# Reordering one step of a chunked recurrence: state products, block products, flags, scans and the decay of the state

## The chip, the cores and the metric

The kernel runs on one core of a Trainium2 chip. The metric is device time in microseconds of one execution. TensorE (PE, with its weight loads PEld), VectorE (DVE), ScalarE (ACT), GpSimd (POOL) and SyncE (SP, which issues nearly all DMAs) each work through their own list of instructions in order and wait for each other through semaphores.

## What is computed

Two stages follow each other. The first is a recurrence over 768 time steps for 4 x 8 heads with a 40 x 40 state each:

```
y[t]  = r[t] @ state
Sa    = state @ a[t]
state = state * w[t]  -  outer(Sa, b[t])  +  outer(v[t], k[t])
```

The second is a mixture of four attention experts on the output of the first (per expert a causal softmax attention of width 64, the two best experts of each token mixed by a gate). The change touches the first stage alone.

## The kernel before

**Chunks and windows.** The recurrence is not run step by step. Time is cut into 24 chunks of 32 (`NC`), and four chunks share one window of decays (`NW` = 6 windows). Within a chunk everything is a matrix product: the state products, a triangular 32 x 32 inverse for each head and chunk (`TT`), and masked products of r, k and v. Between windows the state is rescaled by the decay of a window (`PC`).

**A step.** The main loop runs `n` = 0 to 24 and, in each, walks through the list `MAIN`. Each letter is a method of `chunk(c)`, and the number beside it says for which chunk, counted from n:

```
MAIN = [("g", 0), ("f", -1), ("t", -1), ("k", 1), ("u", 0), ("v", 1), ("y", -1), ("z", -1), ("s", 0), ("w", 0)]
```

- g (L295): state times `AB`, accumulated in PSUM `pg`; ACT evicts it to `GT` (L296).
- f (L310): scores of the chunk before, into `pf`; DVE masks them into `FX` in two halves (L313).
- t (L318): transposed state, evicted by ACT into `SD` (L319).
- k (L276): the next chunk's keys, transposed through `pk`, evicted by ACT into `LS` (L277).
- u (L301): U = inverse times `GT`, into `pu`; ACT evicts it, turned in sign, into `R` in two halves (L303).
- v (L291): V's product for the next chunk, which starts its accumulation in `pg`.
- y (L322, L324): output of the chunk before, 64 products; z (L326) scales it on DVE into `XT`, and every second chunk is stored by DMA (L330).
- s (L336): update of the state in PSUM `ps`; DVE adds the old state (`ST`, L340). In the last chunk of a window DVE then multiplies the sum by `PC` (L345).
- w (L306): U transposed into `pu`, evicted by ACT into `VR` (L307).

PE takes these in the order of the list, so a product whose operand is late holds everything behind it. The state of chunk n, `ST`, is needed by g of the next step. `V1`, `R`, `RX` and `RB` have one buffer each; the loads for the next use are issued right behind the last reader (`LOADS`).

**Side work.** While one window is being run, the next is prepared. After each letter of `MAIN` (its place is counted from 0) the loop runs jobs from a table, `SIDE` (`SIDE1` for the first such window). A key of the table is a step counted from the first step of the window *before* the one that is prepared, and slashes part the ten places. The two halves (0 and 1, sixteen heads each) of a window are prepared apart. The letters are methods of `prep`, `mm` and `invert`:

- w, l, e: loads of `EW`, `EK` (into `KB`) and `EA` (into `AB`) by DMA.
- f, g: two flags on ACT over the decays (L176), each with one activation.
- a, b: suffix scan of the decays on DVE (L179) and what follows from it (L181, L182); s: prefix scan on DVE (L184).
- K, H: the two halves of the scaling of `KB` on POOL (L192); X: scaling of `AB` on POOL (L188). The small letters k and x are the same on DVE.
- m0, m1: the block products (L206) through `pk`, then `GB` and `GK` on DVE (L208, L209) and a mask on POOL (L210).
- L, t, T: the triangular inverses of the 16 x 16 blocks on DVE (L219, 28 small pieces in L227 and L229, L231, L232).
- B, D: operands for two more rounds of products, on ACT (L238); P and Q: these rounds, 128 products each through `pk` (L245), followed by an eviction on ACT (L248) and an addition on DVE (L252).

Window W's P, Q and its addition must be over before u of its first chunk. `START` lists what is done for windows 0 ahead of the loop, `AHEAD` what is then done already for window 1. `items` reads such a line.

In what follows the four steps of a window are called **kind 0 to kind 3** (n modulo 4). In the kernel before, kind 0 holds m0, m1 and L; kind 1 most of t, B and T; kind 2 D and P, and of the window after it the flags and scans of half 0; kind 3 Q, and the scans, flags and scalings of half 1 and the scaling of half 0.

Of the kernel before, what the change touches and what calls it, by code (L numbers as in the profile page):

```python
# [21 lines left out]
NW, NC = 6, 24  # L22

SIDE = {
    -3: "/////////0w",
    -2: "//0f0g0a//0l1l/0b0s1w",
    -1: "0e1e0K0H0X//1f1g1a/1b//1s1K1H1X",
    0: "/////m0/m1//L/t6",
    1: "//t4/t4/t4/t6///t4/TB",
    2: "D/////P",  # L30
    3: "/////Q",
}
START = "x0 0w 0l 0e 1w 1l 1e x1 c0 0a 0b 0f 0g 0k 0s 0x 1a 1b 1f 1g m0 1k 1s 1x x2 m1 L B k0 t28 T D P Q"
AHEAD = "0w 0l 1l 0e 1e"

SIDE1 = {
    0: "//0f0g0a0b0K0H///0s0X1w////1f1g1a1b1K1H",
    1: "/1s1X////m0///m1/L",
    2: "t4/t4/t4/t4/t4/t4/t4//T/B",
    3: "D//P///Q",  # L40
}


# [37 lines left out]
def recurrence(tc, ctx, I, xT, FL, CM, early, tail=None):  # L81
# [80 lines left out]
    def prep(w, a):  # L162
# [26 lines left out]
        def kmul(e, k):  # L189
            for t in two:  # L190
                x = kb[0:104, :, :, t, 32 * k:32 * k + 32]
                e.tensor_tensor(x, x, sv[:, :, 1:33].rearrange("p (x t c) n -> p x t c n", t=2, c=4)[:, :, t], op=OP.mult)  # L192
        return dict(w=lambda: load(EW, "EW"), e=load_a, l=lambda: load(kb.rearrange("p x c t n -> p (x c t n)"), "EK"),
                    f=lambda: flag(0), g=lambda: flag(1), a=suf, b=per, s=pre, x=lambda: amul(V), X=lambda: amul(PL),
                    k=lambda: (kmul(V, 0), kmul(V, 1)), K=lambda: kmul(PL, 0), H=lambda: kmul(PL, 1))

    def mm(w, a):

# [80 lines left out]
    def chunk(c):  # L279
# [45 lines left out]
        def s_z():  # L325
            V.tensor_tensor(xt[:, :, 32 * (cw % 2):32 * (cw % 2) + 32], PF[0:104].rearrange("p (i n) -> p i n", n=32),  # L326
                            SC[w % 3].rearrange("p (i c) n -> p i c n", c=4)[:, :, cw, 0:32], op=OP.mult)
            if cw % 2:
                for r in two:
                    SY.dma_start(xT.rearrange("b (h e) t -> (b h) e t", e=40)[16 * r:16 * r + 16, :, 32 * c - 32:32 * c + 32].rearrange("h e t -> e h t"),  # L330
                                 xt[rows(r)])
        def s_s():
            if c == NC - 1:
                return
            for x, r in heads:
                T.matmul(PS[rows(r), x // 4, 80 * (x % 4):80 * (x % 4) + 80], ls[:, x, r], r2[:, :, x, r], start=True, stop=True)  # L336
            pv = PS[0:104, :, 0:320]
            o, i = (x.rearrange("p (b x) t d -> p b (x t d)", b=2) for x in (st1, st0))
            if c:
                V.tensor_tensor(o, i, pv, op=OP.add)  # L340
            else:
                V.tensor_copy(o, pv)
            if cw == 3:
                o = st1.rearrange("p x t d -> p (x t) d")
                V.tensor_tensor(o, o, PC[(w + 1) % 3][:, :, None].to_broadcast([104, 16, 40]), op=OP.mult)  # L345
# [507 lines left out]
```

## Time and profile before

| | us |
|---|---|
| median of 3 runs | 710.42 (707.84 to 717.12) |
| the profiled execution | 711.22 |
| its span, first to last instruction | 709.4 |
| PE busy | 553.9 (78%) |
| DVE busy | 473.5 (67%) |
| ACT busy | 336.3 (47%) |
| POOL busy | 252.7 (36%) |

The profiled execution took 711.22 us, 1.8 us more than its span. The recurrence fills the first 447 us of the span: the window's set-up up to about 62 us, steps 0 to 3 up to 147.5 us, four full windows of steps up to 403.5 us, and the last window. The second stage takes the remaining 262 us. Sums over the whole span therefore mix stages, and the stages are looked at one by one. PEclk is the clock that was granted to TensorE, as a share of full speed.

### The profile page before, as it was taken

To read this page: it belongs to the slowest core of one execution; us is meant where nothing else is said; L and a number is where in the kernel's file an instruction comes from. 1 tells how busy PE (TensorE), PEld (TensorE's weight loads), DVE (VectorE), ACT (ScalarE), POOL (GpSimd) and SP (SyncE) were. 2 spreads that over 40 slices of the span, in tenths; PEclk is the share of its full clock that TensorE was granted. 3 is DMA by queue.
4 is the path that set the end of the run, shared out by engine and by line. 5 is a ranking of instruction groups with operands and counts; after the bars stand their busy time and mean duration, and the time that the engine had idled before them with its cause. 6 is when DMAs were issued, how large, how long until landed. Compare 5 with 4: busy or idle time off the path is not lost.

```text
span 709.4 us, 26350 instructions
## 1 busy us (share of the span) xinstructions
PE 553.9 (78%) x11497; PEld 506.1 (71%) x11497; DVE 473.5 (67%) x974; ACT 336.3 (47%) x702; POOL 252.7 (36%) x233
## 2 busy tenths in 40 slices
PE   0336573888859787868889998699889988999996
PEld 0325473887859677868778887688779877888784
DVE  8871459448643945673483324599999899689793
ACT  3022413424522641353234345267577777777783
POOL 7500762521262047122610001135545345333640
PEclk9999688889988997998798999999999999999999
DMA  5203423413541462254221262431121212201101
GB/s 164 66 0 86 142 66 109 121 40 91 165 108 42 114 175 63 69 142 128 55 77 40 70 191 73 127 101 46 52 80 41 75 45 57 79 1 45 57 1 61
DMA packets 42268, 57.92 MB, mean 82 GB/s; under 512 B 19808, under 2 KB 33376, under 8 KB 40224
## 3 DMA queue, kind: packets, MB, share of 16 engines
q1 hardware_dynamic: 42000, 56.05, 28.3%
q8 instruction: 92, 1.51, 0.9%
q14 instruction: 32, 0.26, 0.1%
q10 hardware_dynamic: 144, 0.10, 0.1%
HBM read 41.98 MB, written 7.86 MB: 70 GB/s over the span
## 4 chain that ended last, share of the span: by engine, by line
PE 32%; DVE 13%; ACT 4%; issue 4%; DMA 2%; SPq 0%; DVEq 0%; ACTq 0%
PE pt L610 4%; PE ot L735 3%; PE sc L690 3%; PE pt L746 3%; PE pt L720 3%; PE pk L245 3%; DVE m L700 2%; PE pf L322 2%; PE pg L295 2%; PE pf L310 2%; DVE qs L619 2%; ACT P L701 2%; PE pf L324 1%; DVE pt L724 1%; PE ps L318 1%
## 5 line engine op out<-in xcount | busy, mean ns | idle before, releaser
L712 POOL TENSOR_TENSOR P<-P,m 128x128 f32<-128x128 f32 (+2 forms) x96 | 89.2, 950 | 115.7 <-DVE m L708 62.0
L192 POOL TENSOR_TENSOR KB<-KB,SUF 104x512 f32<-104x512 f32 x40 | 54.8, 1401 | 99.5 <-DMA KB<-in_EK 88.4
L307 ACT ACTIVATE VR<-pu 80x1024 f32<-80x1024 f32 x24 | 24.5, 1020 | 132.4 <-PE pu L306 132.4
L701 ACT ACTIVATE P<-sc,m 128x128 f32<-128x128 f32 (+2 forms) x96 | 60.8, 634 | 27.5 <-DVE m L700 17.1
L690 PE MATMUL sc<-ks,qs 128*128 128x384 f32 (+4 forms) x256 | 62.5, 347 | 4.8 <-ACT P L701 2.8
L735 PE MATMUL ot<-pt,vv 128*128 128x256 f32 (+1 forms) x384 | 60.3, 289 | 6.3 <-DVE ots L741 6.1
L188 POOL TENSOR_TENSOR AB<-AB,SC 40x1024 f32<-40x1024 f32 x20 | 44.7, 2233 | 51.0 <-DMA AB<-in_EA 41.8
L724 DVE TENSOR_TENSOR pt<-pt,pt 128x384 fp32r<-128x384 f32 (+1 forms) x96 | 58.9, 618 | 5.3 <-ACT pt L723 3.5
L700 DVE TENSOR_REDUCE m<-sc 128x1 f32<-128x128 f32 (+2 forms) x96 | 58.7, 615 | 0.5
L735 PEld LDWEIGHTS ot<-pt,vv 128*128 128x128 f32 x384 | 50.8, 189 | 10.4 <-DVE ots L741 9.1
L295 PE MATMUL pg<-ST,AB 104*64 104x40 f32 x736 | 29.9, 247 | 34.2 <-DVE ST L340 20.7
L723 ACT ACTIVATE pt<-pt 128x384 fp32r<-128x384 f32 (+1 forms) x96 | 52.0, 544 | 9.8 <-PE pt L720 8.3
L206 PE MATMUL pk<-KB,AB 104*64 104x64 f32 x768 | 30.9, 250 | 32.7 <-DMA AB<-in_EA 19.6
L313 DVE TENSOR_TENSOR FX<-pf,CM 64x512 f32<-64x512 f32 x48 | 32.9, 684 | 35.4 <-PE pf L310 34.9
L720 PE MATMUL pt<-CM,P 128*128 128x128 f32 x336 | 52.9, 275 | 3.8 <-DVE qs L619 2.6
L295 PEld LDWEIGHTS pg<-ST,AB 104*64 104x64 f32 x736 | 27.0, 155 | 37.6 <-DVE ST L340 23.1
L206 PEld LDWEIGHTS pk<-KB,AB 104*64 104x64 f32 x768 | 29.4, 164 | 33.5 <-issue 19.7
L322 PE MATMUL pf<-FX,LS 128*40 128x64 f32 x768 | 48.7, 225 | 1.7 <-issue 1.1
L324 PE MATMUL pf<-RX,SD 80*40 80x64 f32 x736 | 47.2, 222 | 3.1 <-issue 3.1
L690 PEld LDWEIGHTS sc<-ks,qs 128*128 128x128 f32 x256 | 40.3, 190 | 8.3 <-ACT P L701 7.6
L610 PE MATMUL pt<-xh,wq 128*128 128x384 f32 x192 | 42.3, 355 | 4.7 <-DVE qs L619 4.5
L322 PEld LDWEIGHTS pf<-FX,LS 128*40 128x40 f32 x768 | 41.0, 118 | 4.1 <-issue 2.4
(140 smaller groups left out, 1362.3 us busy)
## 6 DMA issues: line engine op xcount, KB each, us to landing
KB<-in_EK SPq DMA_DIRECT2D x24, 320.0 KB
AB<-in_EA SPq DMA_DIRECT2D x24, 320.0 KB
ks<-ks SPq DMA_DIRECT2D x32, 192.0 KB
V<-in_V SPq DMA_DIRECT2D x24, 160.0 KB
R<-in_VX SPq DMA_DIRECT2D x48, 80.0 KB
RX<-in_RX SPq DMA_DIRECT2D x48, 80.0 KB
RB<-in_RB SPq DMA_DIRECT2D x48, 80.0 KB
xT<-XT SPq DMA_DIRECT2D x24, 160.0 KB
```

The source lines that it names most:

```text
L192: e.tensor_tensor(x, x, sv[:, :, 1:33].rearrange("p (x t c) n -> p x t c n", t=2, c=4)[:, :, t], op=OP.mult)
L206: T.matmul(PK[rows(t, 64), x // 2, y:y + 64], ab[:, n], kb[0:104, 4 * a + x, c, t], start=True, stop=True)
L295: T.matmul(pg[rows(t, 64), x], ab[:, 4 * (2 * x + t) + cw], st0[:, x, t], start=False, stop=True, skip_group_check=True)
L322: T.matmul(pf[rows(r), x], ls[:, x, r], FX[:, :, x, r], start=True, stop=c == 0)
L610: T.matmul(p, w, x, start=(j == 0), stop=(j == len(prs) - 1))
L690: T.matmul(ps[:, c, 0:cw], QS[b][:, e, o], KS[b][:, e, z, k], start=(z == 0), stop=(z == 1 and not last), skip_group_check=True)
L700: V.tensor_reduce(m[:, 0, t:t + 1], ps[:, 0:ch, 0:cw], axis=AX.XY, op=OP.max, negate=True)
L701: later(DE, lambda: A.activation(pv, ps[:, 0:ch, 0:cw], AF.Exp, bias=m[:, 0, t:t + 1], accum_out=m[:, 1, t:t + 1]))
L712: PL.tensor_tensor(P[:, 0:n], P[:, 0:n], m[:, 3, t:t + 1].to_broadcast([128, n]), op=OP.mult)
L720: T.transpose(p[:, 128 * y:128 * y + 128], st["P"][t][:, 128 * c:128 * c + 128], ident)
L724: later(DL, lambda: V.tensor_tensor(l, p[:, 0:n], f32(h), op=OP.subtract))
L735: T.matmul(po[:, 128:256] if one else po, VV[b][:, k, e].rearrange("p a b -> p (a b)"), PT[:, 256 * k:256 * k + (128 if one else 256)], st ...
```

## The change

It does five things.

1. In `MAIN`, v moves from behind u to the end of the step.
2. The tables are rewritten: m0 stands behind u, and m1, P and Q stand behind v, at the end of a step; the flags f and g stand behind u (place 5, behind y; ACT's eviction of U is ahead of them); the four long scans of a window get four places in kinds 2, 3 and 0, and one of the scalings of `KB` moves from POOL to DVE (the new letter p); t is done in two pieces of 14.
3. `AHEAD` holds most of the preparation of window 1's half 0, and it stands in front of P and Q of window 0 and of the load of `V1` for chunk 1.
4. At the end of a window, the decay is applied to the old state (new method q, behind y) and to the new part in PSUM apart, and the two are then added.
5. The line numbers behind the insertion move: L336 becomes L342, L340 becomes L349, L345 becomes L333 (twice) and L347.

```diff
 SIDE = {
...
-    0: "/////m0/m1//L/t6",
-    1: "//t4/t4/t4/t6///t4/TB",
-    2: "D/////P",
-    3: "/////Q",
+    0: "1s1H1X////m0/1f1g////m1L",
+    1: "/t14////B///t14",
+    2: "/T////D////P",
+    3: "/////////Q",
...
-AHEAD = "0w 0l 1l 0e 1e"
+AHEAD = "0w 0l 1l 0e 1e 0a 0b 0f 0g 0s 0K 0H 0X 1w"
...
+        def gauge(o, x):
+            V.tensor_tensor(o, x, PC[(w + 1) % 3].rearrange("p (b i) -> p b i", b=2)[:, :, :, None].to_broadcast([104, 2, 8, 40]), op=OP.mult)
+        def s_q():
+            if cw == 3 and c < NC - 1:
+                o, i = (x.rearrange("p (b x) t d -> p b (x t) d", b=2) for x in (st1, st0))
+                gauge(o, i)
...
-            if c:
+            if cw == 3:
+                gauge(pv.rearrange("p b (i d) -> p b i d", d=40), pv.rearrange("p b (i d) -> p b i d", d=40))
+                V.tensor_tensor(o, o, pv, op=OP.add)
+            elif c:
                 V.tensor_tensor(o, i, pv, op=OP.add)
             else:
                 V.tensor_copy(o, pv)
-            if cw == 3:
-                o = st1.rearrange("p x t d -> p (x t) d")
-                V.tensor_tensor(o, o, PC[(w + 1) % 3][:, :, None].to_broadcast([104, 16, 40]), op=OP.mult)
...
-    MAIN = [("g", 0), ("f", -1), ("t", -1), ("k", 1), ("u", 0), ("v", 1), ("y", -1), ("z", -1), ("s", 0), ("w", 0)]
+    MAIN = [("g", 0), ("f", -1), ("t", -1), ("k", 1), ("u", 0), ("y", -1), ("z", -1), ("s", 0), ("w", 0), ("v", 1)]
...
     units[0]["v"]()
+    for f in items(1, AHEAD, None, None) + items(0, "PQ", inv, None):
+        f()
     load_c(1, 0)
-    for f in items(1, AHEAD, None, None):
-        f()
...
                 units[n + d][x]()
+                if x == "y":
+                    units[n]["q"]() if n < NC else None
```

What this does to the order on the engines is seen at three places. On PE, from a step of kind 2 in the steady windows, before (rows without y, which ends just ahead of the first of them in both kernels):

```order
366 L306 MATMUL pu<-CM,R_111 80x64 x16
367 L295 MATMUL pg<-ST_116,AB_98 64x40 x16
368 L310 MATMUL pf<-RB_113,VR_112 64x64 x16
369 L318 MATMUL ps<-CM,ST_117 80x104 x8
370 L276 MATMUL pk<-CM,KB_100 128x104 x8
371 L301 MATMUL pu<-GT_119,TT_106 32x40 x32
372 L291 MATMUL pg<-V_105,GK_103 32x40 x32
373 L245 MATMUL pk<-TT_107,BB_89 64x64 x58
```

and now, from the end of a step of kind 2 into the next step:

```order
404 L342 MATMUL ps<-R_111,LS_109 40x80 x16
405 L306 MATMUL pu<-CM,R_111 80x64 x16
406 L291 MATMUL pg<-V_105,GK_103 32x40 x32
407 L245 MATMUL pk<-TT_107,BB_89 64x64 x58
...
411 L295 MATMUL pg<-ST_117,AB_98 64x40 x16
412 L310 MATMUL pf<-RB_113,VR_112 64x64 x16
```

V's product (L291) and P (L245) stood between u (L301) and y; they now stand between s (L342) and the next g (L295). On ACT, a step of kind 2 before (JK is what the flags write, R the eviction of U):

```order
97 L319 ACTIVATE SD_118<-ps 80x640
98 L176 ACTIVATE JK_90,FL<-EW_82,CM 104x1024 x2
99 L277 ACTIVATE LS_108<-pk 128x640
100 L303 ACTIVATE R_111<-pu 32x640 x2
101 L248 ACTIVATE MT_86<-pk 128x512
102 L307 ACTIVATE VR_112<-pu 80x1024
```

and now:

```order
100 L319 ACTIVATE SD_118<-ps 80x640
101 L277 ACTIVATE LS_108<-pk 128x640
102 L303 ACTIVATE R_111<-pu 32x640 x2
103 L238 ACTIVATE DB_88<-DD_87,CM 128x32x16 x2
104 L176 ACTIVATE JK_90,FL<-EW_82,CM 104x1024
105 L307 ACTIVATE VR_112<-pu 80x1024
106 L248 ACTIVATE MT_86<-pk 128x512
```

The flags, which stood ahead of the evictions of the keys (LS) and of U (R), now stand behind both. On DVE, a step of kind 3 before:

```order
227 L313 TENSOR_TENSOR FX_115<-pf,CM 64x512 x2
228 L179 SCALAR_TENSOR_TENSOR SUF_84<-EW_82,D_81 104x1056
...
231 L252 TENSOR_TENSOR TT_107<-TT_107,pk 128x32x16
232 L184 SCALAR_TENSOR_TENSOR SC_96<-EW_82,D1P_85 104x1056
233 L326 TENSOR_TENSOR XT_120<-pf,SC_97 104x16x32
234 L340 TENSOR_TENSOR ST_116<-ST_117,ps 104x640
235 L345 TENSOR_TENSOR ST_116<-ST_116,PC_92 104x640
```

and now, up to the first DVE work of the next step:

```order
230 L313 TENSOR_TENSOR FX_115<-pf,CM 64x512 x2
231 L184 SCALAR_TENSOR_TENSOR SC_96<-EW_82,D1P_85 104x1056
232 L333 TENSOR_TENSOR ST_116<-ST_117,PC_92 104x640
233 L326 TENSOR_TENSOR XT_120<-pf,SC_97 104x16x32
234 L333 TENSOR_TENSOR ps<-ps,PC_92 104x2x320
235 L347 TENSOR_TENSOR ST_116<-ST_116,ps 104x640
236 L179 SCALAR_TENSOR_TENSOR SUF_84<-EW_82,D_81 104x1056
...
239 L192 TENSOR_TENSOR KB_100<-KB_100,SUF_84 104x16x32 x2
240 L252 TENSOR_TENSOR TT_107<-TT_107,pk 128x32x16
241 L184 SCALAR_TENSOR_TENSOR SC_96<-EW_82,D1P_85 104x1056
```

A scan (L179) and the addition to the inverse (L252) stood ahead of the new state; one scan (L184, of the other half) still does, the rest now follows it, and there is one DVE instruction more at the state (two in L333, one in L347, for two before) and two more for the scaling of `KB` (L192).

More of the change, by code (lines that the diff above doesn't have):

```diff
@@ L24 @@
 SIDE = {
-    -3: "/////////0w",
-    -2: "//0f0g0a//0l1l/0b0s1w",
-    -1: "0e1e0K0H0X//1f1g1a/1b//1s1K1H1X",
-    0: "/////m0/m1//L/t6",
-    1: "//t4/t4/t4/t6///t4/TB",
-    2: "D/////P",
-    3: "/////Q",
-}
-START = "x0 0w 0l 0e 1w 1l 1e x1 c0 0a 0b 0f 0g 0k 0s 0x 1a 1b 1f 1g m0 1k 1s 1x x2 m1 L B k0 t28 T D P Q"
-AHEAD = "0w 0l 1l 0e 1e"
+    -3: "0w/////0f",
+    -2: "///0l1l//0g////0a0b0K0H",
+    -1: "0e1e/0s0X1w///////1a1b1p",
+    0: "1s1H1X////m0/1f1g////m1L",
+    1: "/t14////B///t14",
+    2: "/T////D////P",
+    3: "/////////Q",
+}
+START = "x0 0w 0l 0e 1w 1l 1e x1 c0 0a 0b 0f 0g 0k 0s 0x 1a 1b 1f 1g m0 1k 1s 1x x2 m1 L B k0 t28 T D"
+AHEAD = "0w 0l 1l 0e 1e 0a 0b 0f 0g 0s 0K 0H 0X 1w"
 SIDE1 = {
[L37 to L40, printed above, removed]
+    0: "1a1b1K1H//1s1X//m0/1f1g",
+    1: "////m1/L/t4//t14",
+    2: "/t10T/////B///D",
+    3: "////P/////Q",
 }
@@ L194, in prep @@
                     f=lambda: flag(0), g=lambda: flag(1), a=suf, b=per, s=pre, x=lambda: amul(V), X=lambda: amul(PL),
-                    k=lambda: (kmul(V, 0), kmul(V, 1)), K=lambda: kmul(PL, 0), H=lambda: kmul(PL, 1))
+                    k=lambda: (kmul(V, 0), kmul(V, 1)), p=lambda: kmul(V, 0), K=lambda: kmul(PL, 0), H=lambda: kmul(PL, 1))
     def mm(w, a):
@@ L342, in s_s @@
                 V.tensor_copy(o, pv)
-            if cw == 3:
-                o = st1.rearrange("p x t d -> p (x t) d")
-                V.tensor_tensor(o, o, PC[(w + 1) % 3][:, :, None].to_broadcast([104, 16, 40]), op=OP.mult)
-        return dict(v=s_v, g=s_g, u=s_u, w=s_w, t=s_t, y=s_y, z=s_z, s=s_s, f=s_f)
+        return dict(v=s_v, g=s_g, u=s_u, w=s_w, t=s_t, y=s_y, z=s_z, s=s_s, f=s_f, q=s_q)
     jobs = {}
-    MAIN = [("g", 0), ("f", -1), ("t", -1), ("k", 1), ("u", 0), ("v", 1), ("y", -1), ("z", -1), ("s", 0), ("w", 0)]
+    MAIN = [("g", 0), ("f", -1), ("t", -1), ("k", 1), ("u", 0), ("y", -1), ("z", -1), ("s", 0), ("w", 0), ("v", 1)]
     def at(n, s, *fs):
```

## The prediction

> **What bounds the kernel now.** I cut the span at the starts of g in steps 0, 4, 8, 12, 16 and 20 and asked for each engine's busy time and the granted clock in each stretch. The columns are the length, then the busy time of PE, PEld, DVE, ACT and POOL with the number of instructions, the granted clock, the DMA share and GB/s.
>
> ```profile
> 62.00:147.50 85.50, 50.79 (x1513) 46.91 (x1498) 51.48 (x67) 28.38 (x43) 40.61 (x28) 0.82 0.39 112
> 147.50:212.60 65.10, 51.81 (x1666) 49.13 (x1666) 37.41 (x61) 25.01 (x37) 21.84 (x17) 0.90 0.39 104
> 212.60:277.30 64.70, 51.64 (x1664) 48.56 (x1664) 39.26 (x61) 24.90 (x37) 23.29 (x17) 0.92 0.39 105
> 277.30:343.50 66.20, 53.20 (x1666) 50.35 (x1666) 38.08 (x61) 24.92 (x37) 20.18 (x15) 0.89 0.39 103
> 343.50:403.50 60.00, 54.30 (x1664) 51.25 (x1664) 26.66 (x53) 20.89 (x29) 8.19 (x7) 0.87 0.21 56
> 403.50:447.50 44.00, 37.49 (x1280) 34.34 (x1280) 16.62 (x25) 19.14 (x27) 4.05 (x12) 1.00 0.40 114
> 447.50:709.40 261.90, 235.03 (x1617) 206.66 (x1617) 220.51 (x581) 181.95 (x477) 110.01 (x122) 0.99 0.21 59
> ```
>
> A window of four steps costs 60 to 66 us, with PE busy for 52 to 54 of them and nothing else above 40. So PE's list sets the pace, and it loses time in two ways: by waiting, and by the clock, which is 0.87 to 0.92 there and 1.00 in the last window. The 262 us behind 447.5 belong to the second stage, which the change leaves alone. Next the waits of PE (in sum, times, longest), in the four windows:
>
> ```profile
> PE pg L295 <- DVE ST L345: 13.5, 5, 4.3
> PE pk L245 <- ACT LS L277: 11.0, 6, 2.0
> PE pg L295 <- DVE ST L340: 11.0, 12, 2.0
> PE pk L245 <- issue: 6.8, 6, 2.9
> PE pf L324 <- issue: 3.1, 3, 1.5
> ```
>
> and in steps 0 to 3:
>
> ```profile
> PE pg L295 <- DVE ST L340: 8.6, 1, 8.6
> PE ps L336 <- ACT R L303: 8.0, 2, 7.2
> PE pu L301 <- ACT GT L296: 6.9, 1, 6.9
> PE pk L206 <- POOL AB L188: 3.5, 1, 3.5
> ```
>
> In the windows 24.5 us go to g waiting for the new state (13.5 + 11.0) and 11.0 us to P and Q waiting for the eviction LS, which stands behind two flags on ACT. "issue" is time for which the profile knows no releaser.
>
> The clock falls just behind such waits. Two waits from the order of time, and the stretches at half clock behind them:
>
> ```profile
> 263.47 1.28 PE L245 MATMUL pk<-MT,DB 64*64 64x64 f32 x26 [1.81 <-ACT LS L277]
> 277.33 1.70 PE L295 MATMUL pg<-ST,AB 104*64 104x40 f32 x32 [4.30 <-DVE ST L345]
> 264.00:267.40 3.40, 2.99 (x58) 2.80 (x55) 0.00 (x0) 0.62 (x1) 3.33 (x2) 0.50 0.67 177
> 277.70:284.50 6.80, 6.80 (x128) 6.43 (x127) 1.38 (x2) 1.84 (x3) 1.61 (x1) 0.50 0.10 27
> ```
>
> A wait of 1.81 us is followed by 3.4 us at half clock, one of 4.30 us by 6.8 us, in which PE is busy throughout. From the PEclk column, the time at half clock is 2 x (1 - clock) x length: 13.0 + 10.4 + 14.6 + 15.6 = 53.6 us in the four windows. In the two stretches PE is busy for 88 and 100% of it; with 80 to 90% everywhere, full clock would save 21 to 24 us, and I take 22. [...]
>
> **The price of a step on PE.** A step without side work, with nothing but the letters, in order of time:
>
> ```profile
> 413.66 1.13 PE L295 MATMUL pg<-ST,AB 104*64 104x40 f32 x32 [0.40 <-DVE ST L340]
> 414.62 1.13 PE L310 MATMUL pf<-RB,VR 80*64 80x64 f32 x32
> 415.68 0.91 PE L318 MATMUL ps<-CM,ST 104*80 104x104 f32 x8
> 416.43 0.88 PE L276 MATMUL pk<-CM,KB 104*128 104x104 f32 x8
> 417.23 0.77 PE L301 MATMUL pu<-GT,TT 32*32 32x40 f32 x63
> 417.83 0.79 PE L291 MATMUL pg<-V,GK 32*32 32x40 f32 x63
> 418.55 0.31 PE L322 MATMUL pf<-FX,LS 128*40 128x64 f32 x2
> 420.51 0.23 PE L336 MATMUL ps<-R,LS 128*40 128x80 f32 x1
> 421.90 0.65 PE L306 MATMUL pu<-CM,R 64*80 64x64 f32 x16
> 412.79 0.82 DVE L340 TENSOR_TENSOR ST<-ST,ps 104x640 f32<-104x640 f32 x1 [1.58 <-PE ps L336]
> 415.80 1.41 DVE L313 TENSOR_TENSOR FX<-pf,CM 64x512 f32<-64x512 f32 x2 [2.19 <-PE pf L310]
> ```
>
> From start to start: g 0.96, f 1.06, t 0.75, k 0.80, u 0.60, v 0.72, y 1.96, s 1.39, w 0.65, in sum 8.9 us, and 0.40 of wait for the state. Side work of a window:
>
> ```profile
> 155.69 2.09 PE L206 MATMUL pk<-KB,AB 104*64 104x64 f32 x64
> 182.71 3.91 PE L245 MATMUL pk<-TT,BB 64*64 64x64 f32 x128 [2.05 <-ACT LS L277]
> ```
>
> Less an overlap of 0.2 with what follows, m0 and m1 take 1.9 each; P takes 3.9 here; I take 4.2 for it and for Q, since other instances hold short pauses (6 of them in the list above). A window without any wait at full clock is 4 x 8.9 + 3.8 + 8.4 = **47.8 us**.
>
> **What the edits do, walked through one window.** Prices of the side work, by line (least, median and longest of one in ns, or busy us and mean ns of one):
>
> ```profile
> L345 DVE TENSOR_TENSOR ST<-ST,PC x5: 825/1629/2440, 145.8 to 402.7; 104x640 f32<-104x640 f32 x5
> L184 DVE TENSOR_TENSOR_SCAN SC<-EW,D1P x11: 2350/2358/3404, 14.6 to 337.4; 104x1056 f32<-104x1056 f32 x11
> L192 DVE TENSOR_TENSOR KB<-KB,SUF x8: 651/684/1748, 12.1 to 27.4; 104x512 f32<-104x512 f32 x8
> L219 DVE STREAM_TRANSPOSE MT<-GB 128x1024 f32<-128x1024 f32 x4 | 7.9, 1985 | 0.0
> L227 DVE TENSOR_TENSOR TP<-MT 128x112 f32<-128x112 f32 x12 | 3.3, 273 | 0.4
> L176 ACT ACTIVATE JK<-EW,CM 104x1024 bf16<-104x1024 f32 x22 | 25.2, 1145 | 12.8 <-DMA EW<-in_EW 12.4
> L188 POOL TENSOR_TENSOR AB<-AB,SC 40x1024 f32<-40x1024 f32 x13 | 29.5, 2272 | 31.3 <-DMA AB<-in_EA 28.1 <-PE ps L336 2.7
> ```
>
> *v behind w.* The state needs about 1.0 us behind s (0.82 of L340 and two hand-overs). w alone, 0.65, did not cover it; w and v, 1.37, do, and where P, Q or m1 follow, 2 to 4 us more. The 0.40 of a step without side work goes. Nothing is paid for v's new place: its `V1` load has a whole step either way, and its accumulation in `pg` starts behind GT's eviction.
>
> *Flags behind U's eviction, P and Q at the end.* LS and R no longer wait for two flags (L176, 1.15 us each, with a short read behind each some 2.6), and P and Q no longer stand between U and s. The 11.0 us go. The flags now precede VR on ACT, but w starts 4.0 us behind u's start (u, y and s), and R's two halves, each like a half of L313, end some 2.1 us behind it, which leaves room for one flag and most of the second.
>
> *Decay apart.* The product with the old state runs behind y, beside s. Behind s stand two instructions as before, now with PSUM operands: I take 0.82 each, the price of L340 (the bounds are 0.69, an eviction like half of L313, and the 2.44 of L345 at its longest). That is 1.7 us, and w, v and Q (5.6 us on PE) hide all of it; without that cover it would be the wait of 13.5 us again. A third instruction adds 0.8 us to DVE's list.
>
> *Walk, with 0 at g of kind 1.* An instruction of 512 columns on DVE (L208, L209, z) is taken as half of L313, 0.7, and T as one and a half of L219. L208, L209 and L219 behind m1 end at 3.5, FX at 4.9; y could start at 4.2, so PE **waits 0.8**. The first 14 pieces of t, half of 28 at up to 0.27, end at 8.8, z (0.7) at 9.5, the state at 10.3; s and w, v end at 9.7: **waits 0.7**. Kind 2 starts at 10.4; the second 14 hold DVE to 14.2, FX ends at 15.6, y could start at 14.6: **waits 1.1**. T (3.0) and z end at 19.4, the state at 20.2; P runs until 24.5. Kind 3: FX, the scan (2.4), the decayed old state, z and the two at the state end at 33.5; the next scan, its small followers and p at 38.5; Q at 37.5. Kind 0: the last scan ends at 42, FX at 43.5; m0 takes PE until 43.4: **waits 0.1**. `AB` of half 1 is ready on POOL at 46.5 (two of L188 behind the scan), m1 is due at 48. So: 47.8 + 2.7 = **50.5 us**. To this come the pauses without a releaser (6.8 + 3.1, with the small ones some 12 us in four windows): 3 us each (a little of which is in P's 4.2 already), **53.5**. The last of the four windows has no scans, and I take 51.
>
> *Clock.* Waits of 1.1 us and less: the last window has such ones, and ran at 1.00. I take full clock.
>
> [...]
>
> **The sum.** Four windows: 256.0 us before; 3 x 53.5 + 51 = 211.5 after: **-44.5**. Counter-check by what goes: 24.5 + 11.0 + 22 - 4 x 2.7 = 46.7.
>
> Steps 0 to 3: 85.5 us before. In the old order the loads of window 1 stand behind the load of `V1`, which waits for v; flags, scans and scalings follow late, and the four waits above, 27.0 us, are their price. Now these loads and half 0's work run beside P and Q of window 0. Walking on PE: 4 x 8.9 less what chunk 0 lacks (t, half of y, g: 4), 3.8, 8.4 and some 9 us of waits for half 1's scans and POOL's scalings in steps 0 and 1 give 53. DVE's 51.48, less half 0's scans (5.6) and plus 2.4, gives a floor of 48. PEclk 0.82 says that gaps there bring half clock, so I take 57.5: **-28** (bounds 0, since no load or scan comes later than before, and -37).
>
> Last window: 0.4 x 4: **-2**, rounded. In sum -74.5: 711.2 - 74.5 = 636.7. The median of the runs shown lies 0.8 below the profiled execution, which gives **636 us** (635.9).
>
> **Rivals.**
>
> 1. *DVE becomes the bound.* Its list grows from 39 to 41.7 us per window, and in kinds 3 and 0 it has no gap for 20 us. If scans and scalings are stretched by 1 us each beside POOL (9 instructions, 3.4 instead of 2.36 as in L184's longest), and every stretch lands on y, a window is 60 (the last 58), the start gives 20, and the sum is -18 - 20 - 2: about **670 us**. Against it: in kind 0 m0 covers 1.9 us. [...]
>
> 2. *The waits go, half clock stays.* If gaps of 1 us in succession are enough for it, the 22 us stay and the start gives 24: -22.5 - 24 - 2, **663 us**. Against it stands the last window at 1.00.
>
> 3. *Better still.* Pauses without a releaser shrink, since the products are spread more evenly, and the start reaches its floor: 3 x 51 + 49 and -37: **618 us**.
>
> 4. *Slower: half 1 comes late to m1.* m1, P and Q now stand ahead of g, in the list that carries the state. If POOL's scaling of half 1 (behind EK, EA, two scans, the decay) is later than 48 in the walk, PE stands, and everything with it; the slack is 1.5 us. The 74.5 us would be spent if each of five windows stood for 15 us beyond it. L188's row has 28.1 us of POOL waiting for EA's loads, which is 7 a window, but ahead of half 0's scaling, 12 us before m0. At 20 us per window: 636 + 100, **735 us**.
>
> 5. *Nothing happens.* P, Q, m0 and m1 remain in one list, and if a wait is only carried to the next letter, the time stays at **708**. Against it: every removed wait has work of another engine behind it in the walk.
>
> **Chances and range.** Forecast (625 to 652) 0.55; DVE-bound 0.15; half clock 0.10; better 0.13; nothing 0.04; slower 0.03. The range from 613 to 672 takes in the first four but their outer ends, and leaves out less than 2 in 10. About 2% (14 us) is what a measurement of this kernel can tell from no change: faster by more 0.93, within it 0.04, slower 0.03.
>
> **What would show it.** In the new profile: L245 with no wait for LS; L295's waits for the state near zero in kinds 0 and 3 and below 1 us in kinds 1 and 2; PEclk near 1.00 from step 4 on; windows of 51 to 56 us; step 4 starting at 115 to 125 us; the second stage again at 262. Wrong it would be if y (L322) waits for FX by more than 1.5 us a step, if m1 (L206) waits for `AB`, or if f waits for VR behind the flags.

## The result: 664.7 us, and what the profile after shows

| | before | after |
|---|---|---|
| median in the same comparison, us | 709.84 (707.84 to 717.12) | 664.74 (656.58 to 673.17) |
| ratio after / before, with its 95% interval | | 0.927 (0.914 to 0.940) |
| the profiled execution, us | 711.22 | 656.58 |

The ratio compares the faster executions of each kernel alone, which is why it is not the quotient of the two medians (0.936). By it the kernel is 7.3% faster. 636 us was predicted, with a range from 613 to 672. In a later comparison the changed kernel took 658.42 us (653.25 to 662.11), so a difference of some 6 us between numbers of two comparisons means nothing here.

First the same cut as before, at the starts of g in steps 4, 8, 12, 16 and 20 (columns as in the prediction: length, busy time of PE, PEld, DVE, ACT and POOL, granted clock, DMA share, GB/s). The first row holds steps 0 to 3, the last the second stage:

```profile
60.00:122.70 62.70, 52.42 (x1529) 49.27 (x1526) 41.96 (x64) 24.03 (x34) 28.93 (x20) 0.81 0.35 98
122.70:179.30 56.60, 50.55 (x1667) 47.55 (x1665) 41.15 (x65) 25.84 (x37) 19.96 (x15) 0.94 0.43 120
179.30:230.80 51.50, 47.40 (x1668) 44.66 (x1664) 35.81 (x61) 25.85 (x37) 16.83 (x13) 1.00 0.49 131
230.80:293.90 63.10, 51.78 (x1669) 48.70 (x1666) 41.28 (x65) 25.88 (x37) 19.47 (x14) 0.92 0.41 108
293.90:348.60 54.70, 49.10 (x1667) 46.21 (x1666) 34.13 (x60) 23.61 (x33) 10.10 (x8) 0.97 0.24 64
348.60:390.40 41.80, 36.89 (x1217) 33.87 (x1216) 16.16 (x24) 18.61 (x27) 3.45 (x4) 0.96 0.42 117
390.40:654.70 264.30, 237.73 (x1681) 208.49 (x1681) 221.07 (x584) 182.70 (x478) 110.67 (x131) 0.99 0.21 58
```

Step 4 starts at 122.7 instead of 147.5 us, a gain of 24.8. The four windows take 225.9 instead of 256.0 us, a gain of 30.1. The cut between the last window and the second stage does not fall on the same instruction in both kernels (1217 products ahead of it here, 1280 before), so these two are taken together: 306.1 instead of 305.9 us, no gain. In sum this is 54.7 us between the two profiled executions, and 74.5 were predicted. Of the 19.8 us that are missing, 14.4 lie in the four windows, where 44.5 were expected, 3.2 in steps 0 to 3, and 2.2 in what follows the windows. The median lies another 8 us above the profiled execution (664.74 against 656.58), and no profile shows where. The four windows are not alike: one took 51.5 us at full clock, another 63.1 at 0.92.

The waits of PE in these four windows (sum, times, longest):

```profile
PE pg L291 <- issue: 5.3, 3, 4.2
PE pk L276 <- DVE TT L252: 4.5, 2, 2.3
PE pf L322 <- DVE FX L313: 3.9, 7, 0.7
PE pu L306 <- issue: 3.2, 1, 3.2
PE pg L295 <- DVE ST L349: 2.9, 4, 0.8
PE pk L245 <- issue: 2.9, 3, 1.4
PE ps L342 <- issue: 1.9, 3, 0.9
PE pk L206 <- issue: 0.7, 1, 0.7
PE pu L301 <- issue: 0.7, 1, 0.7
PE pf L310 <- issue: 0.5, 1, 0.5
```

The waits that the change aimed at are gone. The 24.5 us of g for the state have become 2.9, once a window, and P and Q do not wait for LS at all (11.0 before). What is left is mostly "issue", 15.2 us in sum (5.3 + 3.2 + 2.9 + 1.9 + 0.7 + 0.7 + 0.5), and a wait that was not there before: k, 4.5 us, for the addition L252.

**What stands behind "issue".** The longest pause, with the instructions of PE around it in order of time, and the row of the load that SP had issued ahead of it:

```profile
262.62 1.42 SPq L170 DMA_DIRECT2D KB<-in_EK  x4
268.07 0.56 PE L291 MATMUL pg<-V,GK 32*32 32x40 f32 x39
272.87 0.43 PE L291 MATMUL pg<-V,GK 32*32 32x40 f32 x25 [4.24 <-issue]
```

and the stretch behind it, from the windows view (clock 0.50):

```profile
273.40:276.80 3.40, 3.40 (x69) 3.40 (x69) 0.00 (x0) 0.00 (x0) 2.29 (x3) 0.50 0.68 174
```

The pause falls in the middle of v, after 39 of its 64 products. All 64 have the same kinds of operands, and those of the other 25 were there: it is not data that PE lacks. Half clock begins right behind the pause. The page of the profile lists the DMA queues (packets, MB, share of 16 engines), and two of them carry instructions:

```profile
q8 instruction: 92, 1.51, 1.0%
q14 instruction: 32, 0.26, 0.1%
```

q8 is PE's: the same page counts 22,994 products and weight loads (11,497 each), which is 250 for each of its 92 packets. These packets are 16 KB each (1.51 MB in all), and in the trace's DMA records their starts in the recurrence lie about 4 us apart, 52 of them in the four windows. Here are the starts around the pause (us), from these records:

```
253.86  257.68  261.10  270.28  274.60  277.97
```

Between 261.10 and 270.28 none starts for 9.2 us, and in this time, at 262.62, SP issued the load of `EK` (four pieces of 320 KB). PE runs out of its list at 268.6 and goes on 2.6 us after the next packet started. The second longest pause, 3.2 us in w at 168.4, has the same picture: four pieces of `EA` issued from 161.34 on, and no instruction packet from 161.38 to 168.93.

That it is the list that runs out is seen from where the pauses stand. If PE's instructions are counted in the order of the trace (weight loads, products and the waits of its sequencer), all 13 pauses of the list above lie a multiple of 256 instructions apart, to within one. Each stands between two blocks of 16 KB (16,384 bytes, 64 for an instruction), whatever letter is being run, and PE goes on 2.2 to 2.9 us after the start of a packet. A packet starts when PE has begun the block before: 1.1 us later in the median of the four windows, but 5.2 and 4.4 us later at the two longest pauses. A block of side work is passed in 3.9 us (the 128 products of P with their weight loads), so even the usual 1.1 and 2.2 to 2.9 us leave little over. The 12 pauses that the kernel before has in its four windows stand between blocks as well.

**What stands behind k's wait.** SP's issues and DVE's rows from a step of kind 3 into the next, in order of time, and k at the end:

```profile
217.43 1.45 SPq L173 DMA_DIRECT2D AB<-in_EA  x4
220.02 2.36 DVE L184 TENSOR_TENSOR_SCAN SC<-EW,D1P 104x1056 f32<-104x1056 f32 x1
222.44 0.66 SPq L170 DMA_DIRECT2D EW<-in_EW  x2
230.30 2.36 DVE L179 TENSOR_TENSOR_SCAN SUF<-EW,D 104x1056 f32<-104x1056 f32 x1 [3.66 <-DMA EW<-in_EW]
233.02 3.10 DVE L192 TENSOR_TENSOR KB<-KB,SUF 104x512 f32<-104x512 f32 x2
236.04 0.67 DVE L252 TENSOR_TENSOR TT<-TT,pk 128x512 f32<-128x512 f32 x1
236.77 1.65 PE L276 MATMUL pk<-CM,KB 104*128 104x104 f32 x8 [2.32 <-DVE TT L252]
```

`EW` has one buffer, so SP issues the load of its half 1 when the scan 0s (L184) has read half 0, at 222.4. That is behind the four pieces of `EA`, and the scan 1a (L179) stands on DVE for 3.66 us until it has landed. The scaling p and then Q's addition L252 come late by as much, and k, whose PSUM buffer `pk` L252 reads, waits 2.32 us. In the four windows these waits of the scan are 11.5 us (three times), and two of them reach k; before there were none.

### The profile page after: what moved, and what is told of

It is laid out like the page before. It is cut to its first block, busy times and chain, and to the rows that moved or that the text cites. A ratio compares the mean times of both kernels' runs of the same rounds, so it can differ in the third digit from the quotient of the medians.

```text
span 654.7 us, 26365 instructions
## 1 busy us (share of the span) xinstructions
PE 544.8 (83%) x11497; PEld 496.8 (76%) x11497; DVE 480.6 (73%) x987; ACT 340.3 (52%) x702; POOL 241.2 (37%) x225
## 3 DMA queue, kind: packets, MB, share of 16 engines
q8 instruction: 92, 1.51, 1.0%
## 4 chain that ended last, share of the span: by engine, by line
PE 53%; DVE 26%; issue 8%; ACT 5%; DMA 4%; SPq 0%; DVEq 0%; ACTq 0%
PE pk L245 6%; PE ot L743 4%; PE pk L206 4%; PE pt L618 4%; PE pf L322 4%; PE pt L728 3%; PE sc L698 3%; PE pt L754 3%; PE ps L342 3%; PE pf L324 3%; PE pf L310 2%; DVE m L708 2%; PE pg L295 2%; DMA EW<-in_EW 2%; ACT P L709 2%
## 5 line engine op out<-in xcount | busy, mean ns | idle before, releaser
L192 POOL TENSOR_TENSOR KB<-KB,SUF 104x512 f32<-104x512 f32 x32 | 42.9, 1368 | 108.2 <-DVE SUF L179 83.3
L743 PEld LDWEIGHTS ot<-pt,vv 128*128 128x128 f32 x384 | 50.8, 189 | 11.1 <-DVE ots L749 9.2
L188 POOL TENSOR_TENSOR AB<-AB,SC 40x1024 f32<-40x1024 f32 x20 | 44.9, 2245 | 36.0 <-DVE SC L184 16.9
L731 ACT ACTIVATE pt<-pt 128x384 fp32r<-128x384 f32 (+1 forms) x96 | 52.0, 544 | 10.2 <-PE pt L728 8.8
L307 ACT ACTIVATE VR<-pu 80x1024 f32<-80x1024 f32 x24 | 24.5, 1021 | 42.6 <-PE pu L306 42.5
L296 ACT ACTIVATE GT<-pg 128x320 f32<-128x320 f32 x24 | 10.5, 437 | 63.0 <-PE pg L295 63.0
L728 PEld LDWEIGHTS pt<-CM,P 128*128 128x128 f32 x336 | 36.7, 141 | 7.5 <-issue 3.2
```

What stands on the lines that cost most here:

```text
L728: T.transpose(p[:, 128 * y:128 * y + 128], st["P"][t][:, 128 * c:128 * c + 128], ident)
L731: A.activation(h, p[:, 0:n], AF.Copy)
L743: T.matmul(po[:, 128:256] if one else po, VV[b][:, k, e].rearrange("p a b -> p (a b)"), PT[:, 256 * k:256 * k + (128 if one else 256)], st ...
```

## The experiments

The theory on which they were chosen: the sum of the prediction holds part by part, and what is missing comes from the bursts of loads. All times of the first four kernels are from one comparison, in which before took 712.47 us.

**Flags back in their places.**

```diff
-    -3: "0w/////0f",
-    -2: "///0l1l//0g////0a0b0K0H",
-    -1: "0e1e/0s0X1w///////1a1b1p",
-    0: "1s1H1X////m0/1f1g////m1L",
+    -3: "0w",
+    -2: "//0f0g/0l1l//////0a0b0K0H",
+    -1: "0e1e/0s0X1w/1f1g//////1a1b1p",
+    0: "1s1H1X////m0/////m1L",
```

> The changed kernel, with the flags of windows 2 to 5 put back to their old places in kinds 2 and 3, behind t and so ahead of the evictions of the keys (LS) and of U (R); all else as changed. My theory (each edit is worth the waits that it removes): R ends 2.6 us later in kinds 2 and 3; y hides some 0.5 of it, so s (L342) waits about 2 us twice a window, in sum 16 to 20 us in four windows, and s waiting for R stands in the list of PE's waits. Time 680 to 686 against 665. Rival (the list on PE is slack there, since P and Q have left the place between u and s, and y waits anyway): within 4 us of the changed kernel, no wait of s for R above 0.5 us.

Measured: 692.23 us (686.17 to 693.24), ratio 0.972 (0.965 to 0.978). A wait of PE, and one of ACT, over the whole span:

```profile
PE ps L342 <- ACT R L303: 38.7, 7, 12.9
ACT JK L176 <- DMA EW<-in_EW: 40.8, 4, 11.1
```

This is more than expected, and for another reason. In kind 2, where `EW` has landed long before its flags, s waits 0.5 to 1.0 us for R. In kind 3 it waits 11 to 13, since the flag 1f stands on ACT until `EW`'s half 1 has landed, which in the new table is loaded only behind the scan 0s. The run does not price the flags' activations; it shows that, with scans and loads in their new places, the flags cannot stay in their old ones.

**V's product back behind u** (in `MAIN`, with the places in the tables shifted by one).

```diff
-    MAIN = [("g", 0), ("f", -1), ("t", -1), ("k", 1), ("u", 0), ("y", -1), ("z", -1), ("s", 0), ("w", 0), ("v", 1)]
+    MAIN = [("g", 0), ("f", -1), ("t", -1), ("k", 1), ("u", 0), ("v", 1), ("y", -1), ("z", -1), ("s", 0), ("w", 0)]
```

> The changed kernel with v back behind u; every other job keeps its neighbour. My theory: only kind 1 and the steps of the last window have nothing else behind w, so the wait for the state comes back there with 0.4 to 0.7 us each, some 9 steps, plus 4 us; against that y starts 0.7 later and its waits for FX (3.9 us in the windows) go. Net 0 to +4 us, 665 to 669. Rival (v's place is what hides the state in every step): 0.7 us in 23 steps and half clock behind the gaps, 680 or more, with g waiting for the state in all four kinds.

Measured: 671.42 us (667.8 to 676.65), ratio 0.944 (0.936 to 0.953). Waits of PE between 100 and 400 us:

```profile
PE pf L322 <- issue: 15.6, 9, 4.4
PE pf L322 <- DVE FX L313: 11.1, 4, 3.0
PE ps L342 <- issue: 7.5, 4, 5.4
PE pg L295 <- DVE ST L349: 3.4, 7, 0.8
```

v's place alone is worth some 10 us beside the next kernel, where 0 to 4 were expected. The wait for the state is small here too, since m1, P and Q still stand behind s; what grows is y's wait for FX and the pauses. So v behind w pays, but hardly through the wait of g by which the prediction argued; why y waits longer for FX was not followed.

**Decay on the sum again** (sum, then product, as before; no q).

```diff
-            if cw == 3 and c < NC - 1:
+            if False:
...
-            if cw == 3:
-                gauge(pv..., pv...)
-                V.tensor_tensor(o, o, pv, op=OP.add)
-            elif c:
+            if c:
                 V.tensor_tensor(o, i, pv, op=OP.add)
...
+            if cw == 3:
+                o = st1.rearrange("p x t d -> p (x t) d")
+                V.tensor_tensor(o, o, PC[(w + 1) % 3][:, :, None].to_broadcast([104, 16, 40]), op=OP.mult)
```

> The changed kernel with the decay as before the change: the sum of old and new state first, then one product with the decay; no third instruction. My theory: w, v and Q (5.6 us on PE) cover either form, so the time is that of the changed kernel within 3 us (662 to 668), and g does not wait for the state at the start of kind 0. Rival (the product on SBUF beside POOL is stretched to 2.4 us and pushes the scans, p and the addition to the inverse back, for which k waits): k's wait for the addition (L252) grows by 0.8 us a window or more, plus 4 to 8 us.

Measured: 661.39 us (659.24 to 662.51), ratio 0.927 (0.920 to 0.933), the same as with the change's decay. g has no wait at a window's start, and k's wait for L252 is there again (4.9 us). Applying the decay apart neither costs nor brings anything that can be measured: w, v and Q hide either form. Since this kernel runs like the changed one, it serves as its neighbour in this comparison.

**The old start** (P and Q of window 0 and the load of `V1` ahead of `AHEAD`'s work).

```diff
-START = "... k0 t28 T D"
+START = "... k0 t28 T D P Q"
...
-    for f in items(1, AHEAD, None, None) + items(0, "PQ", inv, None):
-        f()
     load_c(1, 0)
+    for f in items(1, AHEAD, None, None):
+        f()
```

> The changed kernel with the start in the old order: P and Q of window 0 first, then v, the load of V for chunk 1, and only then the loads, flags, scans and scalings of window 1's half 0. My theory: this order is worth most of what steps 0 to 3 gained (25 us): the loads of window 1 are issued at about 62 us again, U's eviction waits behind the flags, and step 4 starts at 140 or later instead of 122.7; time 682 to 690. Rival (the table of window 1 is what counts, and the early loads only save the one wait of s for R, 7.2 us): step 4 at 128 to 132, time 670 to 674.

Measured: 672.28 us (671.04 to 676.5), ratio 0.945 (0.938 to 0.952). Waits of PE in steps 0 to 3:

```profile
PE pk L206 <- DMA EW<-in_EW: 9.8, 1, 9.8
PE pu L301 <- ACT GT L296: 7.7, 1, 7.7
```

Step 4 starts at 138.9 us instead of 122.7. So 16 of the 24.8 us come from the order of the loads and side work ahead of step 0, and the remaining 8 to 9 from the other edits in steps 0 to 3. In the whole time 10.9 us are seen beside the neighbour. Its profile and the neighbour's show where the rest is: step 4 starts 15.3 us later (138.9 against 123.6), the four windows are 1.6 us shorter (222.6 against 224.2), and what follows them, which this edit leaves alone, is 5.2 us shorter (307.7 against 312.9). So the theory had step 4 nearly right, and the rival the time.

**No loads of `EK` and `EA`** for windows 2 to 5. The kernel works on what is left in the buffers, so it leaves out a part of the data; every instruction on the engines stays. For this and the next three, before took 711.81 us (703.19 to 717.45).

```diff
-                SY.dma_start(flat(ab[rows(s)]), I["EA"][w, a, s])
+                if w < 2:
+                    SY.dma_start(flat(ab[rows(s)]), I["EA"][w, a, s])
...
-... l=lambda: load(kb.rearrange("p x c t n -> p (x c t n)"), "EK"),
+... l=lambda: load(kb.rearrange("p x c t n -> p (x c t n)"), "EK") if w < 2 else None,
```

> The changed kernel without the loads of EK and EA for windows 2 to 5 (it goes on with the operands of windows 0 and 1; all instructions on the other engines stay). In the changed kernel PE has some 22 us of pauses without a releaser (issue), and the longest (3.2 and 4.2 us) stand where a fetch of PE's instructions (a transfer of 16 KB about every 4 us) started 7.6 and 9.2 us after the last, just behind the 1.3 MB of EA or EK. My theory (PE runs out of instructions because their transfers queue behind these loads): the pauses fall to 8 us or less, no gap of fetches above 6 us in the windows, PEclk there 0.98 or more, time 640 to 650. Rival (the pauses come from the density of PE's own list): 18 us or more of pauses stay, 660 or more.

Measured: 631.18 us (629.96 to 634.1), ratio 0.892 (0.881 to 0.901). The windows, the waits of PE in them, and the scan's wait on DVE (lines are higher by one here):

```profile
114.00:166.20 52.20, 47.60 (x1665) 44.81 (x1664) 41.94 (x65) 25.88 (x37) 20.34 (x16) 1.00 0.30 80
166.20:217.10 50.90, 47.41 (x1668) 44.74 (x1666) 40.72 (x65) 25.84 (x37) 18.89 (x14) 1.00 0.29 82
217.10:269.80 52.70, 48.19 (x1666) 45.03 (x1665) 41.13 (x65) 25.88 (x37) 19.31 (x15) 1.00 0.28 79
269.80:320.40 50.60, 47.41 (x1669) 44.63 (x1666) 32.36 (x57) 23.62 (x33) 9.43 (x8) 1.00 0.26 69
```

```profile
PE pk L246 <- issue: 6.5, 6, 2.0
PE pf L323 <- DVE FX L314: 4.0, 8, 0.7
PE pg L296 <- DVE ST L350: 3.0, 4, 0.8
PE pk L277 <- DVE TT L253: 0.8, 2, 0.4
DVE SUF L180 <- DMA EW<-in_EW: 1.8, 3, 0.8
```

With the loads gone, everything that was missing in the windows is there: full clock in all four, 206.4 us for them, the scan's wait 1.8 instead of 11.5 and k's 0.8 instead of 4.5, the longest gap between two instruction packets 5.06 instead of 9.18 us. No packet starts more than 2.6 us after PE has begun the block before, and the load of `EW` in kind 3 is used 4.1 us after its issue (161.50 against 157.41) where the rows above have 7.9. The waits for FX and for the state are those of the changed kernel, so it is not DVE that ran faster. Pauses of 2 us and less remain in P and Q, 6.5 us (six times), and 0.8 in the block products (twice). Steps 0 to 3 gain as well (step 4 starts at 114.0 us), which is a part of why the time is 9 us below what was expected. This run does not part the two ways in which the loads act (on the instruction packets and on `EW`); both go.

**Halves of `EK` and `EA` loaded apart.**

```diff
-    -2: "///0l1l//0g////0a0b0K0H",
-    -1: "0e1e/0s0X1w///////1a1b1p",
+    -2: "///0l//0g//1l//0a0b0K0H",
+    -1: "0e/0s0X1w////1e///1a1b1p",
```

> The changed kernel with the four large loads apart: EK's half 0 behind k of kind 2 as now, EK's half 1 behind s of kind 2, EA's half 0 behind g of kind 3, EA's half 1 behind y of kind 3. If PE's pauses come from transfers of instructions that queue behind 1.3 MB in one piece, halves of 0.65 MB leave 10 to 14 us of the 22, and the time is 650 to 658. Rival (the bytes count, not the burst, or the pauses have another cause): pauses 18 us or more, 660 to 670. If the later loads come too late for the scalings, PE waits for AB at m1, and the time is above 670.

Measured: 647.99 us (639.88 to 654.55), ratio 0.907 (0.890 to 0.924). The scan's wait for `EW` falls to 4.4 us. Pauses remain, now in P and Q (9.1 us between 100 and 400 us); in time, those in Q follow the load `1e`. The time is below the 650 to 658 of the theory, but the profile does not bear its reason out: the pauses in the four windows are 16.2 us (15.2 in the changed kernel), and the windows take 222.2 us together, where two profiles of the changed kernel have 225.9 and 222.1. What is shorter is the way to step 4, which starts at 117.5 us (122.7 and 121.2). So halves alone do not cure the pauses.

**Q's addition ahead of p.**

```diff
-    -1: "0e1e/0s0X1w///////1a1b1p",
+    -1: "0e1e/0s0X1w///////1a1b/1p",
```

> The changed kernel with DVE's scaling p of kind 3 behind Q and its addition to the inverse (L252), for which k of kind 0 waits 4.5 us in the windows. My theory (k waits because p, 0.7 us an instruction alone and 1.5 beside POOL, stands ahead of the addition): k's wait goes, 3 to 5 us less, 657 to 663. Rival (DVE's list is full in kinds 3 and 0, and the wait only moves to y for FX or m1 for AB): y's or m1's wait grows by as much, time as the changed kernel.

Measured: 657.86 us (654.18 to 660.38), ratio 0.927 (0.915 to 0.940). Two rows, of PE and of DVE:

```profile
PE pf L322 <- DVE FX L313: 6.3, 8, 1.8
DVE SUF L179 <- DMA EW<-in_EW: 15.7, 3, 6.6
```

k's wait is gone, and y waits longer for FX instead (6.3 against 4.6 us between 100 and 400 us), which takes back 1.7 of the 4.5 us. The late scan is still late, by 15.7 us. The time lies in the range of the theory, but the ratio is that of the changed kernel (0.927), so no gain is shown; of the rival, the time held and the wait only in part.

**Both of these.** The tables of the two kernels ahead together.

```diff
-    -2: "///0l1l//0g////0a0b0K0H",
-    -1: "0e1e/0s0X1w///////1a1b1p",
+    -2: "///0l//0g//1l//0a0b0K0H",
+    -1: "0e/0s0X1w////1e///1a1b/1p",
```

> Both edits at once, the loads spread and p behind the addition. If each is worth what its own theory says, 645 to 655; if the pauses or the full list on DVE stay, 660 to 665.

Measured: 652.39 us (648.42 to 659.81), ratio 0.918 (0.902 to 0.934), not told apart from the spread loads alone.

**The changed kernel once more**, beside the last three, as their neighbour (here before took 715.31 us, 704.0 to 722.59).

> The changed kernel once more, as the measure for the next three on the same chip: 657 to 667.

Measured: 658.42 us (653.25 to 662.11), ratio 0.929 (0.921 to 0.936). Its profile (653.41 us) has step 4 at 121.2 us and 222.1 us for the four windows, with 14.3 us of pauses, 3.6 of k's wait and 10.7 of the scan's: the picture of the first one again.

**Spread further**: `EA`'s half 1 behind g of kind 0, behind Q.

```diff
-    -2: "///0l1l//0g////0a0b0K0H",
-    -1: "0e1e/0s0X1w///////1a1b1p",
-    0: "1s1H1X////m0/1f1g////m1L",
+    -2: "///0l//0g//1l//0a0b0K0H",
+    -1: "0e/0s0X1w///////1a1b1p",
+    0: "1e1s1H1X////m0/1f1g////m1L",
```

> The loads of EK and EA apart as before, but EA's half 1 only behind g of kind 0, where no other large load is near. In the first spread version the pauses that were left stood in Q of kind 3, behind EA's two halves. If they come from the burst, Q's pauses (some 4 us a window above its 4.2) go and the time is 640 to 648, 15 to 20 us below the changed kernel on the same chip. Rival (the bytes count): the pauses move to kind 0, 650 to 660. If EA's half 1 comes too late for the scaling, m1 waits for AB.

Measured: 646.05 us (641.46 to 653.06), ratio 0.909 (0.900 to 0.917). Its four windows:

```profile
119.00:174.00 55.00, 49.02 (x1668) 46.30 (x1665) 41.47 (x65) 25.84 (x37) 20.03 (x15) 0.97 0.46 127
174.00:224.80 50.80, 47.35 (x1670) 44.59 (x1666) 36.95 (x61) 25.84 (x37) 16.30 (x12) 1.00 0.49 130
224.80:282.00 57.20, 50.52 (x1668) 47.57 (x1666) 41.73 (x68) 25.85 (x37) 20.38 (x15) 0.94 0.43 120
282.00:332.90 50.90, 47.61 (x1666) 44.59 (x1664) 32.24 (x57) 23.61 (x33) 9.26 (x8) 1.00 0.27 74
```

The same loads at other places make it 12.4 us faster than its neighbour, less than the 15 to 20 that were expected, and the two intervals do not touch. Between the two profiles, which are 10.2 us apart, 8.2 lie in the windows: 213.9 us together instead of 222.1, and two of the four stand at 51 us and full clock. Their pauses are 10.4 us instead of 14.3. With the next one this is the fastest kernel here that loads all its data. The longest gap between instruction packets is 7.0 us.

**In eighths**: each of the eight 320 KB pieces at a place of its own (i and j are the two pieces of a half of `EK`, n and o those of `EA`). POOL's scaling 0X moves behind the piece 0o that it needs.

```diff
-    -2: "///0l1l//0g////0a0b0K0H",
-    -1: "0e1e/0s0X1w///////1a1b1p",
-    0: "1s1H1X////m0/1f1g////m1L",
+    -2: "///0i//0g0j///1i/0a0b0K0H",
+    -1: "0n/1j0s1w////0o0X///1n1a1b1p",
+    0: "1o1s1H1X////m0/1f1g////m1L",
```

> All eight pieces (0.33 MB each) of EK and EA at places of their own, from k of kind 2 to g of kind 0. If a transfer of PE's instructions waits behind what is queued when it is asked for, pauses of at most 1 us are left, 8 to 12 us in all, and the time comes near the version without these loads (631): 634 to 644. Rival (the bytes count, or the many pieces keep the queue always filled): as the spread version or worse, 648 or more.

Measured: 645.61 us (643.68 to 654.67), ratio 0.911 (0.904 to 0.918). No better than the kernel before it, and less than was expected: the longest gap is 8.65 us, the pauses in the four windows are 13.1 us, and the windows take 221.8 us, as in its neighbour (222.1). What its profile gains beside the neighbour's lies ahead of step 4 (117.6 instead of 121.2 us) and behind the windows. So the size of one burst is at most a part of it; what else counts, and whether it is another load, was not tried.

**The flags alone**: the kernel before, with only the flags behind y, and the load of `EW`'s half 1 with them.

```diff
-    -2: "//0f0g0a//0l1l/0b0s1w",
-    -1: "0e1e0K0H0X//1f1g1a/1b//1s1K1H1X",
+    -2: "//0a//0l1l/0b0s/0f0g1w",
+    -1: "0e1e0K0H0X//1a/1b//1s1K1H1X/1f1g",
```

> The kernel before, with one part of the change alone: the flags of half 0 and half 1 stand behind y (and so behind the eviction of U) in kinds 2 and 3; the load of EW's half 1 goes with them. My theory: the wait of P and Q for LS (11.0 us) goes, and with it the half clock behind it in kind 3 (some 1.7 us a window); the waits for the state stay. 695 to 701 against 710. Rival (the wait only moves: P and Q then wait for nothing, but s or g take it up): 706 to 712.

Measured: 706.57 us (699.41 to 711.43), ratio 0.993 (0.988 to 0.998). The waits of PE between 100 and 400 us:

```profile
PE pg L295 <- DVE ST L340: 21.4, 13, 8.9
PE pk L245 <- issue: 12.2, 8, 4.5
PE pg L295 <- DVE ST L345: 9.5, 4, 2.6
```

P and Q no longer wait for LS, but by the ratio only about 5 us are gained (0.7% of 715), less than the 11.0 us of that wait and than was expected. The pauses of P and Q are 12.2 us here, and g still waits for the state. In its own four windows (146.4 to 401.3 us, as long as before: 255.0 against 256.0) PE's pauses are 20.0 us, where before had 11.9. So most of the removed wait came back as pauses. The time is that of the rival, but its reason (s or g takes the wait up) did not show.

## Why the prediction was right, and where it missed

**The number: inside the range, outside the forecast's own band.** 664.7 us lies above the 625 to 652 that the forecast had a chance of 0.55 for, and in the part of the range that was added for the rivals. It stands beside rival 2's 663, but for another reason than rival 2 gave, and about 8 us of it are the distance of the median from the profiled execution. That it falls there is chance; what the parts below show is what was right.

**Bounds and direction: right.** PE's list set the pace, and the two waits that the change removes fell as walked: g for the state from 24.5 (1.2 of it just ahead of step 4) to 2.9 us (0.7 once a window was predicted), LS from 11.0 to nothing. y waits for FX 3.9 us, never over 0.7 at once; the walk had 0.8 + 1.1 + 0.1 a window, 8 in all. m1 and f have no wait for `AB` or VR that shows in the four windows.

**The start: right, a little high.** 24.8 us were measured where 28 were taken. The old start put back takes 15 to 16 of them away. "PEclk 0.82 says that gaps there bring half clock" held (0.81 now), with 8.5 us of waits and pauses in three places, which end at 71.5, 102.1 and 85.7 us, and 6.8, 6.8 and 10.2 us at half clock right behind them (from 72.0, 102.7 and 85.7 us):

```profile
PE pg L295 <- DVE ST L351: 3.2, 1, 3.2
PE pg L291 <- issue: 3.1, 1, 3.1
PE pg L295 <- DVE ST L349: 2.2, 1, 2.2
```

**Decay apart: right.** Nothing gained, nothing lost, shown by the kernel with the old form. The three instructions took what was assumed (0.80 to 0.83 us each).

**Last window: 2 us predicted, none seen.** g's waits for the state went (2.3 us before, none now), but PE's pauses are 3.4 us there instead of 2.6 and the clock is 0.96 instead of 1.00. Cut at the same instruction (PE's wait for the second stage's tile `fl`, L757 before and L765 now), it takes 45.4 instead of 44.1 us, and the second stage 260.7 instead of 261.8.

**The four windows: 225.9 instead of 211.5 us.** Here the steps failed, by 14.4 us:

- *"3 us each" for pauses without a releaser.* The prediction took them as a property of PE's list, 9.5 us over the four windows. They are 15.2. All stand where a block of instructions ends, the two longest with the next packet held back behind loads of 1.3 MB, and the kernel without these loads has 6.5 in P and Q and 0.8 elsewhere. In the list with fewer waits the packets follow each other sooner: in the four windows they start 4.4 us apart (median) before and 4.0 now. That the same delay shows more for this reason is the author's reading; no run shows it by itself.
- *"I take full clock."* From the clock of the four windows, 2 x (0.06 x 56.6 + 0.08 x 63.1 + 0.03 x 54.7) = 20 us are at half clock; what is left of the 14.4 us after the other three points (+5.7, +4.5, -4.0) puts their price at 8 us. The four stretches at half clock begin at 171.0, 235.9, 273.4 and 300.7 us: at or behind the two longest pauses and k's two waits (2.2 us and more each), not behind many small waits: without the loads, four windows with eight waits for FX of 0.7 us and less, four for the state of 0.8 and less, and pauses up to 2.0 all ran at 1.00. So in these windows the argument from the last window held, and rival 2 (half clock from small gaps) did not; what failed is that no long gap would be left. In the last window itself 3.4 us at half clock now follow a pause of 1.34 us (at 382.3), so the length of one wait does not tell by itself where the clock falls.
- *k was not in the walk.* k now comes behind Q's addition, and waits 4.5 us for it. The walk let the scan 1a start when DVE was free; it was the load of `EW` that set it, 11.5 us in sum, issued only when the scan 0s was over and behind `EA`, which the prediction had not followed. Without the loads k waits 0.8.
- On the other side, the waits for FX and the state are 6.8 us together, where 4 x 2.7 = 10.8 were taken.

191.2 us (4 x 47.8, no wait) + 6.8 + 4.5 + 15.2 + 8.2 of half clock make up the 225.9, the last term being the rest. The windows without long gaps are 50.6 to 52.7 us (51.5 in the changed kernel, 50.8 and 50.9 with spread loads), where the walk without pauses had 50.5: its prices for the steps were right.

**The rivals.** DVE did not become the bound: its busy time is 34 to 41 us a window. A stretch beside POOL, on which rival 1 rested, is seen in this row of p:

```profile
L192 DVE TENSOR_TENSOR KB<-KB,SUF x16: 648/1505/1748, 12.2 to 296.7; 104x512 f32<-104x512 f32 x16
```

Half of the instructions take 1.5 us and more, where the median of before was 0.68; the eight of p take 1.50 to 1.67 us each, all of them while POOL runs its own scalings of `KB` (L192). But that is 0.8 us on two instructions in a window, and no gain is shown from Q's addition ahead of p. The scans of the four windows (L179, L184) took 2.34 to 2.36 us each, none of them beside a scaling on POOL, and the decayed old state (L333) 0.80 to 0.83, three times of four with POOL's L188 running: neither was stretched. Why p is stretched is not shown. "Nothing happens" held in part for the flags alone, where the removed wait came back as pauses.

## What to carry to other kernels

When waits are taken out of an instruction list, look in the profile at what they had covered: here PE's own instructions, which come by DMA in packets of 16 KB, and one small load issued behind four large ones. A pause without a releaser can be tested by counting: if such pauses stand a block of instructions apart (here 13 pauses, each a multiple of 256 from the next, to within one), it is the list that has run out. Spread large prefetches over the steps, and keep them from going out just ahead of a small load that somebody waits for; the same bytes at other places were worth 12 us of 658, though only one of the three ways of spreading them shortened the windows. And when one part of a larger change is undone as a test, follow its loads first: the flags put back waited for a load that had moved with another part.

## What was not expected of the hardware

Instruction packets of PE start some 4 us apart in a dense list of small products (median 4.0 us in the four windows), and behind 1.3 MB of loads a gap grew to 9.2 us, with a pause of 4.24 us on PE and 3.4 us of half clock behind it. The block size is seen twice in the trace: packets of 16,384 bytes, and pauses a multiple of 256 instructions apart. The transfers are not hidden here: at 13 of some 52 ends of blocks in the four windows PE paused, for 15.2 us in all, and without the large loads still for 7.3. Leaving out the loads brought the time from 658 to 665 us down to 631. Why a small packet waits for so long behind the loads, and why pieces of 320 KB one by one do not cure it, stays open.
